# Packed attention and a gated MLP on one core: another order for the first three batches, w_out scaled on VectorE, w_in cast on GpSimd

## The chip, the cores and the metric

The kernel runs on one core of a Trainium2 chip. Its engines work side by side, each through its own queue in order, and wait for one another by semaphores: TensorE (PE: matmuls and transposes; weight loads are shown as PEld), VectorE (DVE), ScalarE (ACT), GpSimd (POOL) and SyncE (SP, which here issues the DMAs). The metric is device time in microseconds, the median of several runs. A profiled execution tells where the time goes.

## What is computed

```python
def sm_attn(qq, kk, vv):
    s = scale * np.matmul(qq, kk.transpose(0, 1, 3, 2))      # scale = 1/8
    a = np.exp(s - np.max(s, axis=-1, keepdims=True))
    return np.matmul(a / (np.sum(a, axis=-1, keepdims=True) + 1e-09), vv)

p_packed = sm_attn(p, k, v)                # q, k, v: 8 batches, 8 heads, 576 x 64; p: 32 x 64 per head
out = sm_attn(q, p_packed, p_packed)       # 576 x 64 per head
x = out.transpose(0, 2, 1, 3).reshape(4608, 512)
h = x @ w_in                               # w_in 512 x 2048
g = h * (1.0 / (1.0 + np.exp(-beta * h)))  # beta: 2048
result = g @ w_out                         # w_out 2048 x 512, all float32
```

Each head's 32 packed rows attend over the 576 rows of k and v; then the 576 rows of q attend over the 32 packed rows. The heads side by side are the 4608 x 512 input of an MLP with a gated activation.

## The kernel before

The work goes batch by batch; matmuls are in bf16 with float32 sums. A batch has 512 rows (the main part) and a remainder of 64, and two batches share a tile of 128 remainder rows.

**Attention of a batch.** `load` (L70) brings k, q or v of a batch to SBUF as float32: one DMA for the main part, two for the remainder. `cast` (L84) makes bf16 of it. `transpose_main` (L95) does 16 transposes on PE into PSUM and one copy on DVE (L104); `transpose_rem` (L109) does the remainders of k and q. `scores1` (L131) gives the scores of p against k and their exp on ACT, `packed` (L159) the sums and the packed rows with their division on DVE. `scores2` (L198) gives the scores of q against the packed rows and exp (L212); `norm2` (L215) sums them, and ACT takes Ln and Exp for the reciprocal; `weights2` (L227) multiplies on DVE and makes A2T.

**MLP of a batch.** `fused_w` (L234), in four blocks n of 512 columns, multiplies the packed rows with w_in, and DVE multiplies the result by beta into W (L249). So h is W against A2T: `mlp_main` (L257), 16 feature tiles of two 512-column matmuls and one Silu on ACT each; `mlp_rem` (L268) does the remainder in two halves. `second` (L290) is the product with w_out: for each of 4 tiles of rows (5 for odd batches) 16 accumulating matmuls, a copy on DVE (L303) and a store. It is a generator: each step is one matmul, and `fill(n)` in `phase` puts n of its steps between other work on PE.

**Phases.** `phase(i)` (L471) holds the MLP mains of batch i, the attention of batch i+1 and, as fill, `second` of batch i-1. It also casts batch i+2 on Pool (`refill`, L484) and then loads batch i+3 into the buffer that came free (each of k, q, v has one float32 and one bf16 buffer). After phase 7 `second(7)` follows alone.

**The opening** is written by hand in `run` (L417). p and beta come by ACT's DMA queue, everything else by SP's. `prepare_p` (L347) doubles p and transposes it; `prepare_beta` (L366) guards beta against zero, takes 1/beta (`rbeta`), and spreads beta over all partitions by 16 float32 matmuls in two halves (`brow_ps`, L385; copies on ACT, L390). w_in and w_out come in four blocks of 1 MB each through a pool `stage` of two buffers (L42), which p32 uses as well. DVE casts each w_in block to bf16 (L400); Pool multiplies each w_out block by rbeta into bf16, in four pieces of 512 columns (L412). The order of `run` sets the order in each queue:

```python
o3 = self.load_w_out(3)      # L457; loads on SP's queue
self.cast_w_out(2, o2)       # Pool
self.cast_w_out(3, o3)
for x in "kqv":
    self.load(1, x)          # L461, SP
for x in "kqv":
    self.cast(1, x, pcopy)   # L463, Pool
```

PSUM for attention, transposes and W is a pool `ps_a` of two buffers that all of them take in turn (`att`, L65); mains use two of `ps_h`, `second` two of `ps_o`.

Of the kernel before, what the change touches and what calls it, by code (L numbers as in the profile page):

```python
# [21 lines left out]
NC = 4  # L22
# [8 lines left out]
class Kernel:  # L31
# [3 lines left out]
    def __init__(self, ctx, tc, q, k, v, p, w_in, w_out, beta, out):  # L35
# [6 lines left out]
        self.stage = pool("stage", 2)  # L42
# [41 lines left out]
    def cast(self, b, x, copy):  # L84
        t = self.x32.pop((b, x))
        o = self.inbf.tile([128, 2304], bf16, tag=f"{x}bf", name=f"{x}_bf")
        copy(  # L87
            o[:, 0:2048].rearrange("p (t h d) -> p h t d", t=4, h=8),
            t[:, 0:2048].rearrange("p (h t d) -> p h t d", h=8, t=4),
        )  # L90
        copy(o[:, 2048:2304], t[:, 2048:2304])
        self.xbf[b, x] = o


    def transpose_main(self, b, x):  # L95
        ps = self.att(f"{x}T_ps", bf16)
        src = self.xbf[b, x]
        for c in range(NC):
# [190 lines left out]

    def second(self, b):  # L290

        nc = self.nc
        for t in range(4 + b % 2):
            ps = self.ps_o.tile([128, DM], f32, tag="o", name="o_ps")
            for ft in range(FT):
                lhsT = (
                    self.g[b][:, ft, 128 * t : 128 * t + 128] if t < 4 else self.grem[b // 2][:, ft, :]
                )
                self.mm(ps[:], lhsT, self.w_out_bf[:, ft, :], start=(ft == 0), stop=(ft == FT - 1))
                if ft < FT - 1:  # L300
                    yield
            o = self.op.tile([128, DM], f32, tag="o_sb", name="o_sb")
            nc.vector.tensor_copy(o[:], ps[:])  # L303
            if t < 4:
                rows = self.out[S * b : S * b + SM, :].rearrange("(p t) n -> p t n", t=4)
                nc.sync.dma_start(rows[:, t, :], o[:])
            else:
                for e in range(2):
                    lo = S * (b - 1 + e) + SM
                    nc.sync.dma_start(self.out[lo : lo + SR, :], o[64 * e : 64 * e + 64, :])  # L310
            yield
# [159 lines left out]
    def phase(self, i):  # L471
# [64 lines left out]
        for _ in w2:  # L536
            pass
# [48 lines left out]
```

## Time and profile before

| | us |
|---|---|
| median of 3 runs (lowest to highest) | 333.84 (333.37 to 334.16) |
| the profiled execution | 333.31 |
| its span, first to last instruction | 331.5 |
| PE busy | 257.6 (78%) |
| ACT busy | 167.7 (51%) |
| DVE busy | 120.4 (36%) |
| POOL busy | 77.4 (23%) |
| mean granted TensorE clock | 0.912 of full speed |

Busy time is that of instructions on the engine; register, branch and semaphore work isn't counted. Matmuls are pipelined, so the mean duration of one is longer than its share of a stream. The granted clock is given as a share of 2.4 GHz: 1.00, or 0.50 for 1.2 GHz. The strip of 40 slices has 8.3 us to a slice, and a digit is the busy share in tenths. In the chain that ended last each step is followed back to what released it.

### The profile page before, as it was taken

The page shows a single profiled execution, that of the slowest core. Times are in us where ns is not written, and L with a number is a line of the kernel's source. Part 1 is how long each engine was busy: PE and PEld are TensorE (multiplying, and loading weights), DVE is VectorE, ACT ScalarE, POOL GpSimd, SP SyncE. Part 2 cuts the span into 40 slices and gives each one's busy share as a digit, 9 for nine tenths or more (in the row PEclk, how much of TensorE's full clock was granted, in tenths as well). Part 3 has the DMA queues.
Part 4 walks back from the last instruction along what each step waited for, and adds up shares of the span by engine and source line. Part 5 has one row for each costly group of instructions (what it writes and reads, how often), then busy time and mean ns, then how long its engine had stood idle before and what let it go on. Part 6 is the DMA issues. An engine that isn't in the chain of part 4 may idle for free.

```text
span 331.5 us, 5201 instructions
## 1 busy us (share of the span) xinstructions
PE 257.6 (78%) x2188; PEld 134.7 (41%) x2225; DVE 120.4 (36%) x155; ACT 167.7 (51%) x242; POOL 77.4 (23%) x69
## 2 busy tenths in 40 slices
PE   0297320006659999999999999999999999999994
PEld 0196100005315544643464365345534543544541
DVE  1433760002225228435433651374236427201111
ACT  1024230000986877587458757862886687443300
POOL 3030008999520520440043005200510000000000
PEclk9999555555969999999999999999999999999999
DMA  8960553599994492097029606912010010111122
GB/s 207 300 237 2 170 203 133 180 339 300 296 291 134 140 296 91 34 304 219 32 49 304 205 34 165 313 47 65 32 44 33 22 65 32 41 56 63 47 83 63
DMA packets 49607, 47.01 MB, mean 142 GB/s; under 512 B 16288, under 2 KB 40880, under 8 KB 49584
## 3 DMA queue, kind: packets, MB, share of 16 engines
q1 hardware_dynamic: 47488, 46.15, 46.8%
q10 hardware_dynamic: 2096, 0.53, 0.9%
q8 instruction: 17, 0.28, 0.4%
q14 instruction: 6, 0.05, 0.1%
HBM read 37.23 MB, written 9.44 MB: 141 GB/s over the span
## 4 chain that ended last, share of the span: by engine, by line
PE 71%; ACT 7%; POOL 7%; DMA 5%; issue 4%; DVE 4%; DVEq 0%; POOLq 0%
PE o_ps L58 34%; PE h_ps L58 18%; POOL w_out_bf L412 7%; PE w_ps L58 4%; DMA p<-in_p_dram 3%; PE kT_ps L63 3%; PE qT_ps L63 3%; PE pp_ps L58 3%; ACT E2T L212 2%; PE brow_ps L58 2%; ACT g_main L266 2%; DMA w_out<-in_moe_w_out_dram 2%; PE z_ps L58 1%; DVE w_in_bf L400 1%; PE s_ps L58 1%
## 5 line engine op out<-in xcount | busy, mean ns | idle before, releaser
L58 PE MATMUL o_ps<-w_out_bf,g_main 128*128 128x512 bf16 x496 | 131.7, 380 | 1.7 <-issue 0.5
L266 ACT ACTIVATE g_main<-h_ps 128x512 bf16<-128x512 f32 x128 | 75.8, 597 | 99.3 <-PE h_ps L58 89.5
L58 PE MATMUL h_ps<-A2T,W_bf 128*128 128x64 bf16 (+1 forms) x494 | 83.7, 288 | 1.2 <-ACT g_main L266 0.7
L58 PEld LDWEIGHTS <-g_main 128*128 128x128 bf16 x512 | 47.9, 98 | 55.6 <-issue 2.7
L303 DVE COPY o_sb<-o_ps 128x512 f32<-128x512 f32 x36 | 24.9, 692 | 103.8 <-PE o_ps L58 103.8
L58 PEld LDWEIGHTS <-W_bf 128*128 128x128 bf16 x512 | 31.1, 98 | 28.3 <-issue 8.3
L249 DVE TENSOR_TENSOR W_bf<-w_ps,beta_bc 128x1024 bf16<-128x1024 f32 x32 | 38.4, 1221 | 10.0 <-PE w_ps L58 9.1
L87 POOL CAST k_bf<-k 128x2048 bf16<-128x2048 f32 x7 | 13.2, 1892 | 97.1 <-issue 81.2
L412 POOL TENSOR_SCALAR w_out_bf<-w_out,rbeta 128x512 bf16<-128x512 f32 x16 | 24.7, 1563 | 31.1 <-DMA w_out<-in_moe_w_out_dram 31.1
L63 PE MATMUL kT_ps<-identr,k_bf 128*128 128x128 bf16 x128 | 10.1, 243 | 27.4 <-POOL k_bf L87 27.3
L104 DVE COPY kT<-kT_ps 128x2048 bf16<-128x2048 bf16 x8 | 9.8, 1225 | 44.5 <-PE kT_ps L63 44.5
L63 PEld LDWEIGHTS <-k_bf 128*128 128x128 bf16 x144 | 10.8, 110 | 31.8 <-POOL k_bf L87 28.2
L58 PE MATMUL w_ps<-w_in_bf,pp 64*32 64x512 bf16 x256 | 14.6, 434 | 11.7 <-DVE w_in_bf L400 10.7
L126 ACT ACT_TABLE_LOAD x15 | 19.2, 1283 | 4.8 <-issue 4.6
L129 ACT ACT_TABLE_LOAD x15 | 19.2, 1283 | 0.3
L87 POOL CAST q_bf<-q 128x2048 bf16<-128x2048 f32 x8 | 15.1, 1894 | 15.1 <-DMA q<-in_q_dram 15.1
L186 DVE RECIPROCAL rz<-pp_ps 128x128 f32<-128x128 f32 x8 | 7.7, 958 | 29.0 <-PE pp_ps L58 29.0
L87 POOL CAST v_bf<-v 128x2048 bf16<-128x2048 f32 x7 | 13.3, 1893 | 20.3 <-issue 18.5
L58 PEld LDWEIGHTS <-pp 64*32 64x32 bf16 x384 | 5.0, 90 | 29.7 <-issue 17.5
L58 PE MATMUL o_ps<-w_out_bf,g_rem 128*128 128x512 bf16 x62 | 14.0, 379 | 0.1
L212 ACT ACTIVATE E2T<-s_ps 128x1024 bf16<-128x1024 f32 (+1 forms) x16 | 9.6, 648 | 6.0 <-PE s_ps L58 5.9
L223 ACT ACTIVATE rz<-z_ps 128x1024 f32<-128x1024 f32 (+1 forms) x16 | 9.5, 648 | 6.2 <-PE z_ps L58 4.0
(60 smaller groups left out, 188.2 us busy)
## 6 DMA issues: line engine op xcount, KB each, us to landing
k<-in_k_dram SPq DMA_DIRECT2D x8, 1024.0 KB, 6.6
v<-in_v_dram SPq DMA_DIRECT2D x8, 1024.0 KB, 8.1
q<-in_q_dram SPq DMA_DIRECT2D x8, 1024.0 KB, 8.6
out_dram<-o_sb SPq DMA_DIRECT2D x32, 256.0 KB, 2.4
w_in<-in_moe_w_in_dram SPq DMA_DIRECT2D x4, 1024.0 KB, 6.4
w_out<-in_moe_w_out_dram SPq DMA_DIRECT2D x4, 1024.0 KB, 5.3
k<-in_k_dram SPq DMA_DIRECT2D x16, 64.0 KB, 6.5
v<-in_v_dram SPq DMA_DIRECT2D x16, 64.0 KB, 6.5
```

Of the source, the lines that this page charges most:

```text
L58: return self.nc.tensor.matmul(out, lhsT, rhs, start=start, stop=stop, tile_position=pos, skip_group_check=True)
L63: return self.nc.tensor.matmul(out, in_, ident, is_transpose=True, skip_group_check=True)
L87: copy(o[:, 0:2048].rearrange("p (t h d) -> p h t d", t=4, h=8), t[:, 0:2048].rearrange("p (h t d) -> p h t d", h=8, t=4),)
L104: self.nc.vector.tensor_copy(xT[:, :, 0:SM], ps[:].rearrange("p (c n) -> p c n", c=NC))
L126: self.nc.scalar.preload_act_table_set(EXP_SET)
L129: self.nc.scalar.preload_act_table_set(SILU_SET)
L212: nc.scalar.activation(E[:, :, lo:hi], ps[:, :, 0 : hi - lo], AF.Exp, scale=SCALE)
L223: nc.scalar.activation(rz[:, :, lo:hi], ps[:, :, 0 : hi - lo], AF.Ln)
L249: self.nc.vector.tensor_tensor(W[:, :, cols], ps, self.beta_bc[:, cols].unsqueeze(1).to_broadcast([128, 2, 512]), ALU.mult,)
L266: self.nc.scalar.activation(self.g[b][:, ft, :], ps[:], AF.Silu)
L303: nc.vector.tensor_copy(o[:], ps[:])
L412: self.nc.gpsimd.tensor_scalar_mul(self.w_out_bf[:, ft, :], t[:, i, :], self.rbeta[:, ft : ft + 1])
```

## The change

- **Loads.** p's buffer is taken from the pool `gp`, `stage` has three buffers, and beta is sent ahead of p. The main parts of k, q and v of batch 0 come in that order, each in two DMAs, then three blocks of w_in at once, the fourth behind the cast of the first, then k, q and v of batch 1, then the blocks of w_out. Two of these are emitted behind the first attention, two behind the last W block; batch 2 follows.
- **Opening of batch 0.** The beta work stands ahead of p's, and its second half (`spread_beta(1)`) behind `packed(0)`. Casts of k, q and v are split in heads between DVE and ACT, the remainder on Pool; the copies of p's, k's and q's transposes are split between DVE and ACT.
- **Weights.** w_in blocks 0 to 2 are cast by Pool, block 3 half by DVE and half by Pool. w_out is scaled by DVE.
- **Batches 0 to 2.** Phases 0 and 1 are written out in `run`. The mains of batch 0 run between its last W blocks; then comes the attention of batch 1 without fill; `second(0)` starts in it, with its first two row tiles interleaved by blocks of w_out, and stands between the mains of batch 1. The attention of batch 2 has 46 steps of `second(1)` as fill; phase 2 takes over its other 34.
- **Phases 2 to 7.** k's transposes stand behind main 2 and q's behind main 4 (before: behind mains 0 and 1). The casts and the loads stand at the head of the phase, with the cast for the batch whose attention is in the same phase.

```diff
--- before.py
+++ after.py
-        self.stage = pool("stage", 2)
+        self.stage = pool("stage", 3)
...
-    def load(self, b, x):
+    def load(self, b, x, parts=1):
...
-        nc.sync.dma_start(
-            t[:, 0:2048].rearrange("p (h e) -> p h e", h=8),
-            src[b, :, 0:SM, :].rearrange("h (p t) d -> p h (t d)", p=128),
-        )
+        n = 8 // parts
+        for i in range(parts):
+            h = slice(n * i, n * i + n)
+            nc.sync.dma_start(
+                t[:, 0:2048].rearrange("p (h e) -> p h e", h=8)[:, h],
+                src[b, h, 0:SM, :].rearrange("h (p t) d -> p h (t d)", p=128),
+            )
...
-    def cast(self, b, x, copy):
+    def cast(self, b, x, *copies):
...
-        copy(
-            o[:, 0:2048].rearrange("p (t h d) -> p h t d", t=4, h=8),
-            t[:, 0:2048].rearrange("p (h t d) -> p h t d", h=8, t=4),
-        )
-        copy(o[:, 2048:2304], t[:, 2048:2304])
+        main = copies[:-1]
+        n = 8 // len(main)
+        for i, copy in enumerate(main):
+            h = slice(n * i, n * i + n)
+            copy(
+                o[:, 0:2048].rearrange("p (t h d) -> p h t d", t=4, h=8)[:, h],
+                t[:, 0:2048].rearrange("p (h t d) -> p h t d", h=8, t=4)[:, h],
+            )
+        copies[-1](o[:, 2048:2304], t[:, 2048:2304])
...
-    def transpose_main(self, b, x):
+    def transpose_main(self, b, x, copies=None):
...
-        self.nc.vector.tensor_copy(
-            xT[:, :, 0:SM], ps[:].rearrange("p (c n) -> p c n", c=NC)
-        )
+        copies = copies or [self.nc.vector.tensor_copy]
+        n = NC // len(copies)
+        for i, copy in enumerate(copies):
+            c = slice(n * i, n * i + n)
+            copy(xT[:, c, 0:SM], ps[:].rearrange("p (c n) -> p c n", c=NC)[:, c])
...
     def second(self, b):
 
-        for t in range(4 + b % 2):
-            ps = self.ps_o.tile([128, DM], f32, tag="o", name="o_ps")
-            for ft in range(FT):
-                lhsT = (
-                    self.g[b][:, ft, 128 * t : 128 * t + 128] if t < 4 else self.grem[b // 2][:, ft, :]
-                )
-                self.mm(ps[:], lhsT, self.w_out_bf[:, ft, :], start=(ft == 0), stop=(ft == FT - 1))
-                if ft < FT - 1:
-                    yield
...
+        groups = [[0, 1], [2], [3]] if b == 0 else [[t] for t in range(4 + b % 2)]
+        for group in groups:
+            ps = {t: self.ps_o.tile([128, DM], f32, tag="o", name="o_ps") for t in group}
+            for n in range(4):
+                for t in group:
+                    for ft in range(4 * n, 4 * n + 4):
+                        self.second_mm(b, t, ft, ps[t])
+                        if ft < FT - 1:
+                            yield
+                    if n == 3:
+                        self.second_out(b, t, ps[t])
+                        yield
...
-        self.p32 = self.stage.tile([128, 16, 64], f32, tag="stage", name="p32")
+        self.b16 = self.const.tile([16, 128], f32, name="b16")
+        nc.scalar.dma_start(self.b16[:], self.beta.rearrange("(f p) -> f p", p=128))
+        self.p32 = self.gp.tile([128, 16, 64], f32, tag="grem", name="p32")
         nc.scalar.dma_start(
             self.p32[:], self.p.rearrange("b (g h) j d -> (h j) (b g) d", g=2)
         )
-        self.b16 = self.const.tile([16, 128], f32, name="b16")
-        nc.scalar.dma_start(self.b16[:], self.beta.rearrange("(f p) -> f p", p=128))
...
-        for r in range(2):
+        for r, copy in enumerate((nc.vector.tensor_copy, nc.scalar.copy)):
             h = slice(64 * r, 64 * r + 64)
-            nc.vector.tensor_copy(
+            copy(
...
-        for half in range(2):
-            ps = self.att("brow_ps")
...
-            nc.scalar.copy(self.beta_bc[:, 1024 * half : 1024 * half + 1024], ps[:])
+        self.b_safe = bs
+
+    def spread_beta(self, half):
+        ps = self.att("brow_ps")
...
+        self.nc.scalar.copy(self.beta_bc[:, 1024 * half : 1024 * half + 1024], ps[:])
...
-    def cast_w_in(self, n, t, copy):
-        copy(self.w_in_bf[:, :, 512 * n : 512 * n + 512], t[:])
+    def cast_w_in(self, n, t, *copies):
+        m = NC // len(copies)
+        for i, copy in enumerate(copies):
+            c = slice(m * i, m * i + m)
+            copy(self.w_in_bf[:, c, 512 * n : 512 * n + 512], t[:, c])
...
-            self.nc.gpsimd.tensor_scalar_mul(
+            self.nc.vector.tensor_scalar_mul(
                 self.w_out_bf[:, ft, :], t[:, i, :], self.rbeta[:, ft : ft + 1]
             )
...
     def run(self):
         nc = self.nc
-        vcopy, scopy, pcopy = nc.vector.tensor_copy, nc.scalar.copy, nc.gpsimd.tensor_copy
-        self.load(0, "k")
+        dve, act, pool = nc.vector.tensor_copy, nc.scalar.copy, nc.gpsimd.tensor_copy
         self.load_small()
-        self.load(0, "v")
-        self.load(0, "q")
+        self.load(0, "k", 2)
+        self.load(0, "q", 2)
+        self.load(0, "v", 2)
+        w = [self.load_w_in(n) for n in range(3)]
+        self.exp_set()
         self.constants()
-        self.exp_set()
+        self.prepare_beta()
+        self.spread_beta(0)
+        self.cast(0, "k", dve, act, pool)
         self.prepare_p()
-        self.prepare_beta()
-        w = self.load_w_in(0)
-        self.cast(0, "k", vcopy)
-        self.transpose_main(0, "k")
-        self.cast(0, "v", scopy)
-        self.cast(0, "q", pcopy)
-        self.transpose_main(0, "q")
+        self.transpose_main(0, "k", [dve, act])
+        self.cast(0, "q", dve, act, pool)
+        self.transpose_main(0, "q", [dve, act])
         self.transpose_rem(0)
         self.scores1(0)
+        self.cast(0, "v", dve, act, pool)
+        self.cast_w_in(0, w[0], pool)
+        w.append(self.load_w_in(3))
+        for x in "kqv":
+            self.load(1, x)
         self.packed(0)
-        w1 = self.load_w_in(1)
-        self.cast_w_in(0, w, vcopy)
+        self.spread_beta(1)
+        self.scores2(0)
         self.fused_w(0, 0)
-        self.scores2(0)
-        w2 = self.load_w_in(2)
-        self.cast_w_in(1, w1, vcopy)
+        self.cast_w_in(1, w[1], pool)
+        self.norm2(0)
         self.fused_w(0, 1)
-        self.norm2(0)
         self.weights2(0)
         self.silu_set()
-        w3 = self.load_w_in(3)
-        self.cast_w_in(2, w2, vcopy)
+        wo = [self.load_w_out(0), self.load_w_out(1)]
+        self.cast_w_in(2, w[2], pool)
+        for ft in range(4):
+            self.mlp_main(0, ft)
         self.fused_w(0, 2)
-        o0 = self.load_w_out(0)
-        self.cast_w_in(3, w3, vcopy)
+        self.cast_w_in(3, w[3], dve, pool)
+        for ft in range(4, 8):
+            self.mlp_main(0, ft)
         self.fused_w(0, 3)
-        o1 = self.load_w_out(1)
-        self.cast_w_out(0, o0)
-        o2 = self.load_w_out(2)
-        self.cast_w_out(1, o1)
-        o3 = self.load_w_out(3)
-        self.cast_w_out(2, o2)
-        self.cast_w_out(3, o3)
+        wo += [self.load_w_out(2), self.load_w_out(3)]
         for x in "kqv":
-            self.load(1, x)
-        for x in "kqv":
-            self.cast(1, x, pcopy)
+            self.cast(1, x, pool, pool)
         for x in "kqv":
             self.load(2, x)
-        for i in range(B):
-            self.phase(i)
-        for _ in self.second(B - 1):
-            pass
-
-    def phase(self, i):
-        w2 = self.second(i - 1) if i > 0 else iter(())
+        for ft in range(8, 12):
+            self.mlp_main(0, ft)
+        self.transpose_main(1, "k")
+        for ft in range(12, 16):
+            self.mlp_main(0, ft)
+        self.mlp_rem(0, 0)
+        self.mlp_rem(0, 1)
+        self.transpose_main(1, "q")
+        self.transpose_rem(1)
+        self.exp_set()
+        self.scores1(1)
+        self.packed(1)
+        self.scores2(1)
+        w2 = self.second(0)
+        self.cast_w_out(0, wo[0])
+        self.fused_w(1, 0)
+        self.norm2(1)
+        self.silu_set()
+        self.fill(w2, 8)
+        self.weights2(1)
+        self.fused_w(1, 1)
+        self.cast_w_out(1, wo[1])
+        for ft in range(4):
+            self.mlp_main(1, ft)
+            self.fill(w2, 1)
+        self.fill(w2, 4)
+        self.fused_w(1, 2)
+        self.cast_w_out(2, wo[2])
+        for ft in range(4, 8):
+            self.mlp_main(1, ft)
+        self.fused_w(1, 3)
+        self.cast_w_out(3, wo[3])
+        self.fill(w2, 8)
+        for ft in range(8, 12):
+            self.mlp_main(1, ft)
+        for ft in range(12, 16):
+            self.mlp_main(1, ft)
+            self.fill(w2, 4)
+        self.mlp_rem(1, 0)
+        self.fill(w2, 4)
+        self.mlp_rem(1, 1)
+        for x in "kqv":
+            self.cast(2, x, pool, pool)
+        for x in "kqv":
+            self.load(3, x)
+        self.fill(w2, 99)
+        w2 = self.second(1)
+        self.fill(w2, 2)
+        self.transpose_main(2, "k")
+        self.fill(w2, 6)
+        self.transpose_main(2, "q")
+        self.fill(w2, 6)
+        self.transpose_rem(2)
+        self.exp_set()
+        self.scores1(2)
+        self.fill(w2, 8)
+        self.packed(2)
+        self.fill(w2, 8)
+        self.scores2(2)
+        self.fill(w2, 8)
+        self.norm2(2)
+        self.silu_set()
+        self.fused_w(2, 0)
+        self.fill(w2, 4)
+        self.fused_w(2, 1)
+        self.weights2(2)
+        self.fused_w(2, 2)
+        self.fill(w2, 4)
+        self.fused_w(2, 3)
+        for i in range(2, B):
+            self.phase(i, w2 if i == 2 else self.second(i - 1))
+        self.fill(self.second(B - 1), 99)
+
...
+    def phase(self, i, w2):
         nb = i + 1
...
         def refill(x):
+            if nb < B:
+                self.cast(nb, x, pcopy, pcopy)
             if nb + 1 < B:
-                self.cast(nb + 1, x, pcopy)
-            if nb + 2 < B:
-                self.load(nb + 2, x)
+                self.load(nb + 1, x)
+
+        for x in "kqv":
+            refill(x)
 
...
         main(0, 2)
+        main(1, 2)
+        main(2, 2)
         attn("transpose_main", nb, "k")
-        main(1, 2)
-        attn("transpose_main", nb, "q")
-        main(2, 2)
-        attn("transpose_rem", nb)
-        refill("k")
-        refill("q")
         main(3, 2)
         main(4, 2)
+        attn("transpose_main", nb, "q")
         main(5, 1)
+        attn("transpose_rem", nb)
         attn("exp_set")
         attn("scores1", nb)
         attn("silu_set")
         fill(14)
         main(6, 2)
         attn("packed", nb)
-        refill("v")
...
```

## Rows read from the trace of the kernel before

**Rows 1.** The page, part 2: busy tenths and granted clock of TensorE, 40 slices.
```profile
PE   0297320006659999999999999999999999999994
...
PEclk9999555555969999999999999999999999999999
```

**Rows 2.** Chain that ended last, in order of time: start, us, what.
```profile
0.71 9.78 DMA p<-in_p_dram
...
11.87 1.90 PE pT_ps L63 x16
...
17.10 7.01 PE brow_ps L58 x32
...
42.90 1.36 DVE A2T L229
...
45.42 5.32 DMA w_out<-in_moe_w_out_dram
...
50.92 21.07 POOL w_out_bf L412 x14
...
77.47 1.89 PE kT_ps L63 x16
```

**Rows 3.** Timeline, SP queue: start, us, engine, line, operation, names, count.
```profile
63.71 0.50 SPq L73 DMA_DIRECT2D k<-in_k_dram  x1
```

**Rows 4.** Windows: stretch, length, busy PE, PEld, DVE, ACT, POOL, clock, DMA, GB/s.
```profile
5.00:11.00 6.00, 0.00 (x0) 0.00 (x0) 0.48 (x1) 0.86 (x1) 0.00 (x0) 1.00 1.19 285
...
17.00:21.00 4.00, 4.00 (x20) 4.00 (x20) 2.88 (x3) 0.27 (x1) 2.87 (x2) 1.00 1.04 389
...
60.00:70.00 10.00, 0.00 (x0) 0.00 (x0) 0.00 (x0) 0.00 (x0) 10.00 (x8) 0.50 0.72 253
...
77.40:82.80 5.40, 5.12 (x38) 4.19 (x40) 2.07 (x2) 0.60 (x1) 4.72 (x6) 0.50 1.09 306
```

**Rows 5.** Timeline of the opening: start, us, engine, line, operation, idle before.
```profile
16.64 1.89 POOL L87 CAST q_bf<-q 128x2048 bf16<-128x2048 f32 x1 [13.03 <-DMA q<-in_q_dram]
...
17.31 2.30 DVE L87 CAST k_bf<-k 128x2048 bf16<-128x2048 f32 x1
...
18.48 1.40 POOL L91 CAST q_bf<-q 128x256 bf16<-128x256 f32 x1
...
25.06 1.90 ACT L87 CAST v_bf<-v 128x2048 bf16<-128x2048 f32 x1
...
28.95 0.63 PE L58 MATMUL s_ps<-pT,kT 128*128 128x64 bf16 x16 [0.89 <-DVE qT L104]
...
32.76 0.96 DVE L186 RECIPROCAL rz<-pp_ps 128x128 f32<-128x128 f32 x1 [3.46 <-PE pp_ps L58]
...
34.39 1.23 DVE L400 CAST w_in_bf<-w_in 128x2048 bf16<-128x2048 f32 x1
...
36.07 0.65 PE L58 MATMUL s_ps<-qT,pp 64*32 64x512 bf16 x8
```

**Rows 6.** Groups by form, 136 to 310 us: busy, mean ns | idle before.
```profile
L266 ACT ACTIVATE g_main<-h_ps 128x512 bf16<-128x512 f32 x94 | 56.1, 597 | 52.6 <-PE h_ps L58 45.6 <-PE qT_ps L63 3.5 <-PE w_ps L58 1.5
...
L249 DVE TENSOR_TENSOR W_bf<-w_ps,beta_bc 128x1024 bf16<-128x1024 f32 x20 | 24.0, 1221 | 0.8
...
L303 DVE COPY o_sb<-o_ps 128x512 f32<-128x512 f32 x27 | 18.7, 692 | 79.3 <-PE o_ps L58 79.3
...
L104 DVE COPY qT<-qT_ps 128x2048 bf16<-128x2048 bf16 x5 | 6.1, 1225 | 2.7 <-PE qT_ps L63 2.7
```

**Rows 7.** Windows of phases 1 and 2 (columns as in rows 4).
```profile
104.75:133.80 29.05, 28.24 (x263) 14.36 (x267) 13.13 (x16) 20.84 (x31) 6.66 (x6) 1.00 0.54 151
...
133.80:166.20 32.40, 31.43 (x279) 15.81 (x282) 13.82 (x17) 20.95 (x31) 6.66 (x6) 1.00 0.51 151
```

**Rows 8.** Timeline of phase 1: the table loaded for Silu.
```profile
124.87 1.28 ACT L129 ACT_TABLE_LOAD   x1
```

**Rows 9.** Chain in order of time: the tail.
```profile
310.96 10.74 PE o_ps L58 x49
```

More of the change, by code (lines that the diff above doesn't have):

```diff
@@ L288, in mlp_rem, with second_mm, second_out @@
         )
-    def second(self, b):
-        nc = self.nc
-        for t in range(4 + b % 2):
-            ps = self.ps_o.tile([128, DM], f32, tag="o", name="o_ps")
-            for ft in range(FT):
-                lhsT = (
-                    self.g[b][:, ft, 128 * t : 128 * t + 128] if t < 4 else self.grem[b // 2][:, ft, :]
-                )
-                self.mm(ps[:], lhsT, self.w_out_bf[:, ft, :], start=(ft == 0), stop=(ft == FT - 1))
-                if ft < FT - 1:
-                    yield
[L302 to L311, printed above, removed]
+    def second_mm(self, b, t, ft, ps):
+        lhsT = self.g[b][:, ft, 128 * t : 128 * t + 128] if t < 4 else self.grem[b // 2][:, ft, :]
+        self.mm(ps[:], lhsT, self.w_out_bf[:, ft, :], start=(ft == 0), stop=(ft == FT - 1))
+    def second_out(self, b, t, ps):
+        nc = self.nc
+        o = self.op.tile([128, DM], f32, tag="o_sb", name="o_sb")
+        nc.vector.tensor_copy(o[:], ps[:])
+        if t < 4:
+            rows = self.out[S * b : S * b + SM, :].rearrange("(p t) n -> p t n", t=4)
+            nc.sync.dma_start(rows[:, t, :], o[:])
+        else:
+            for e in range(2):
+                lo = S * (b - 1 + e) + SM
+                nc.sync.dma_start(self.out[lo : lo + SR, :], o[64 * e : 64 * e + 64, :])
+    def second(self, b):
+        groups = [[0, 1], [2], [3]] if b == 0 else [[t] for t in range(4 + b % 2)]
[10 more added lines that the diff above has]
+                        yield
     def constants(self):
@@ L380, in prepare_beta @@
         nc.vector.reciprocal(self.rbeta[:], pc[:, 0:16])
[L381 to L390 removed]
+        self.b_safe = bs
+    def spread_beta(self, half):
+        ps = self.att("brow_ps")
+        for i in range(8):
+            f = 8 * half + i
+            self.mm(
+                ps[:, 128 * i : 128 * i + 128],
+                self.ident32[0:16, f : f + 1].to_broadcast([16, 128]),
+                self.b_safe[:],
+            )
+        self.nc.scalar.copy(self.beta_bc[:, 1024 * half : 1024 * half + 1024], ps[:])
     def load_w_in(self, n):
@@ L473, in phase, with fill @@
+        self.fused_w(2, 2)
[4 more added lines that the diff above has]
+        self.fill(self.second(B - 1), 99)
+    def fill(self, work, n):
+        for _ in range(n):
+            if next(work, self) is self:
+                break
+    def phase(self, i, w2):
         nb = i + 1
@@ L476, in fill @@
         def fill(n):
-            for _ in range(n):
-                next(w2, None)
+            self.fill(w2, n)
         def attn(f, *a):
@@ L535, in phase @@
         self.mlp_rem(i, 1)
-        for _ in w2:
-            pass
+        fill(99)
 @with_exitstack
```

7 lines of the change are left out of this document (removed).

## Prediction

> **What bounds the kernel now.** I read the strip of 40 slices first. TensorE (PE) is at nine tenths in nearly every slice after 104 us, and there is a pit before: from 33 to 83 us it does almost nothing at the lower granted clock [rows 1]. So the kernel has two parts: an opening that waits and seven phases that are PE-bound. In phase 1 PE is busy 28.24 of 29.05 us, in phase 2 31.43 of 32.40 [rows 7]; nothing on other engines can shorten those much. (A window there begins at the phase's first transposes; the phase itself begins with a main, 0.9 us before.)
>
> The chain of waits names what fills the opening [rows 2]: p's landing (10.5 us), 7.0 us of fp32 matmuls that spread beta, w_in casts up to A2T (44.3), then the first w_out block and 21.07 us of Pool scaling w_out, 14 pieces at 1.5 us, and only then batch 1's cast and the transposes at 77.5. The SP queue says why batch 1 is so late: the fourth w_out load waits for a buffer that Pool frees, and k of batch 1 is queued behind it, issued at 63.71 [rows 3]; while Pool held the queue, DMA ran at 253 GB/s and PE at nothing [rows 4]. Phase 0's order puts batch 1's transposes after main 0, so 15 of 16 mains of batch 0, whose A2T was ready at 44.3, wait until after 77. That hole is what the change can take away.
>
> **The change part by part.** Times are of the profiled span (331.5 us).
>
> *Loads.* In the old order k, v, p and q, 4.06 MB, are in when Pool's q cast starts at 16.64 [rows 5]. k, q and v are 1.18 MB each; at 285 GB/s [rows 4] the last of them took 4.1 us, so with q second q is in at about 12.5. v takes 16.6. w_in comes at up to 389 GB/s [rows 4], 1.05 MB in 2.7 to 3.7 us: the blocks land at about 20, 23, 27 and 30 (the fourth needs only Pool's cast of the first). Batch 1 follows (34, 38, 42) and w_out 0 to 2 (46, 49, 52). A landing is on the path only for p and q.
>
> *Opening to the first main.* p still lands at 10.5 to 11 (beta is sent ahead of it, 8 KB). Doubling and transposing p took 10.5 to 13.8; I take 14.3. The beta spread is halved and, if beta lands before 7, lies in front of p for nothing. k's transposes follow at once (1.89, to 16.2 [rows 2]), copied by DVE and ACT in halves (of 1225 ns [rows 6], so 0.6; on ACT 1.0, half of its 1.90 cast of 2048 columns [rows 5]: 17.1); q's cast in halves 1.0 (18.1), transposes 1.9 (20.0), copy 1.0 (21.0). Scores 1 to the end of packed's matmuls took 28.95 to 32.76 [rows 5], 3.8; ACT now also casts half of v there (1.0): 25.7. The second half of the beta spread, 7.0 / 2 = 3.5 us [rows 2], now stands in PE's queue between packed and scores 2; it covers the 1.6 us of DVE work there and costs 1.9: 29.2. From scores 2 to A2T's end took 36.1 to 44.3, 8.2, with a w_in cast of 1.23 [rows 5] on DVE in it, which goes to Pool, and partly hidden: 7.7. First main at **36.9** (7.4 earlier), its successors unblocked.
>
> *DVE and Pool side by side.* The old trace has one overlap: k's cast on DVE took 2.30 us while Pool cast q, against 1.23 for w_in's cast of the same size with Pool idle, and Pool's 256-column piece took 1.40, where its 2048 columns took 1.89 [rows 5]. The Trainium skill, "SBUF — State Buffer", on the port pair that VectorE and GpSimd share, says one side blocks fully while the other holds it; those two rows agree. By that rule each of the casts shared by DVE and Pool (k, q, v, the fourth w_in block) could add up to 1.1 us; on the path it could hit two, and the sum would be 2 us higher. I take 0 to 2 us and put 0 in the sum, since Pool's share is small pieces. Pool's cast of a w_in block lies between its 1.89 for 2048 columns [rows 5] and 4 x 1.5 for the scaling [rows 2]; even 6 us a block ends at 42, ahead of need, so it costs nothing.
>
> *Batch 0's MLP, 36.9 to 51.* Sixteen mains at 0.43 PE (two matmuls at 0.22 [rows 9]) or 0.86 at the lower clock, ACT 0.60 each [rows 6]. The clock rose at 82.8, after PE had been busy 5.12 of 5.40 us [rows 4]; I let the first six mains run at 0.86 (5.2), ten at 0.60 (6.0), two W blocks 1.0, k's transposes 0.9, two remainders 1.2: end 51.2.
>
> *Attention of batch 1 without filler.* q's transposes end at 52; s1 needs q's copy 1225 ns [rows 6], 53.3; then 3.3 to packed's end, 1.6 DVE, s2 and exp: second(0) gets its first fill only behind norm2, at about 61.6. Of these 10 us some 3 are work, so 7 stay lost; I let the clock fall in it and the next 5 us run at half speed (8 fills 3.4 instead of 1.7).
>
> *w_out on DVE.* Four pieces a block; the unknown price of a piece is between 1.23 / 4 = 0.3 and the 0.69 of a 512-column PSUM copy [rows 5, 6]; I take 0.4, 1.6 a block. Blocks 0 and 1 stand in front of W multiplies (1.22 each [rows 6]), and fills wait for block 1 (to 68.5); at 0.69 this adds 2 us. Blocks 2 and 3 are covered by mains. The fourth load waits for block 0's scaling (59.5) and lands 5.3 us later [rows 2], before its need at 75; batch 2's loads behind it land by 75, need 89.
>
> *Second(0) with MLP 1.* From 61.6: 8 fills 3.4; W and mains with block 1 to 70.4; W, four mains, W 3.2; 8 fills 1.8; four mains 2.4; four mains with 16 fills 5.2; two remainders and 24 fills 6.1: **89.3**. Then second(1) is opened and 46 of its 80 fills go beside batch 2's attention: 46 x 0.219 + 6.4 of attention matmuls + 1.3 stalls at the W multiplies: phase 2 starts at **107** (old 133.0, the piece before the transposes at 133.8).
>
> *Phase 2* has 34 fills left instead of 80. Up to scores 2 it uses the 32 it always used; then ACT sets the pace. In phase 1, begun at 103.9, the silu table was loaded by 126.15 [rows 8], 22.2 us on, with nothing before it that the missing fills shorten; eight silus at 0.60 follow [rows 6]: 27.0 instead of 32.4 [rows 7], 5.4 off.
>
> *Phases 2 to 6, moved transposes.* q's transposes now stand one main ahead of scores 1; its PSUM buffer is free after DVE's 1225 ns copy, PE arrives after 0.65 + 0.23: 0.4 to 0.5 us of stall per phase, 2.0 in four phases (phase 2's is in the 27). Moving casts and loads to the head of the phase costs nothing: their inputs are done in the phase before, and output stores are queued behind loads that don't wait. Between 0 (hidden) and 0.9 per phase.
>
> **Sum.** Phase 3 begins at 134 instead of 165.3: 331.5 - 31.3 + 2.0 = 302.2 us of span. The profiled execution took 333.31, 1.8 over its span: 304.0; the median of the runs is 0.5 above it: **304.5 us**.
>
> **Rivals.**
> *The opening is slower than my chain* (0.24, about 311): the clock falls again in batch 2's attention (2.7), mains run at 0.86 longer (3), DVE pieces at 0.69 (2). For: in the slice from 91.2 to 99.5 the clock was down again for part of it, between two at full, in an attention with few fills [rows 1]. Against: after that it never fell.
> *The opening is faster* (0.16, about 299): beta is in early, DMA runs at 389 GB/s throughout, s1's stall is hidden behind fills, the clock is up by 40. Each is worth 1 to 2 us.
> *The loads bind instead* (0.07, about 309): if batch 1 and w_out move at 253 GB/s or less [rows 4], batch 1 lands 4 us later and w_out 2 to 3 some 5 later, which pushes scores 1 and the first fills.
> *Clock stuck, slower than before* (0.02, 370): if pauses between mains, fills and attention keep the granted clock at its lower level from 37 until phase 3, the 65 to 75 us of PE work there double. It needs over 30 us of such work at half speed to lose the whole gain; the strip shows it up for good from 100 us on [rows 1].
> *The change does not do what it says* (0.01, 334): batch 1's loads again stuck behind a weight load. They now stand ahead of w_out and behind the fourth w_in block, whose buffer Pool frees at 22.
>
> **How the numbers follow.** The forecast case has 0.50. The range 297 to 315 holds it with its bounds (unknown DVE pieces +2, port +2, moved transposes -2 to +2) and most of the slower and faster openings and the loads. A measurement tells 0.2%, 0.7 us, from no change: faster 0.97, within 0.01, slower 0.02.
>
> **What would show it.** PE's strip has no empty slices between 37 and 51; batch 1's k is issued before 32; the first fill stands at 58 to 65; phase 2's start near 107, phase 3's near 134; a phase from 3 on 0.4 to 0.5 us longer; Pool's w_in cast near 1.9; a DVE w_out piece near 0.4. Wrong would be: a first main after 42, a second(0) that waits for w_out landings, or steady phases longer by over 1 us.

## The result and the profile after

| | before | after |
|---|---|---|
| median of 4 runs (lowest to highest), us | 334.0 (333.37 to 334.23) | 305.76 (305.26 to 308.15) |
| profiled execution, its span | 333.31, 331.5 | 305.92, 304.1 |
| PE, DVE, ACT, POOL busy | 257.6, 120.4, 167.7, 77.4 | 261.4, 126.0, 165.4, 60.2 |

The ratio is 0.9172 (95%: 0.9122 to 0.9221): faster by 28.2 us, against a forecast of 304.5. A second set of the same two kernels on another chip, used below, gave 307.29 (306.35 to 308.92) against 333.76, so differences of 1 to 2 us between runs of different chips tell little. The work on PE is nearly the same; where it stands is not. The page of after, from its part on busy tenths (answering [rows 1]; a slice is now 7.6 us):

```profile
span 304.1 us, 5209 instructions
...
PE   2768496587999889689999999999999999999993
...
POOL 3136550015206206202600152005200000000000
...
PEclk9999999789999999989999999999999999999998
```

The three empty slices in the pit are gone; what is left is one at 4 tenths just ahead of the first main (30 to 38 us) and one at 5 tenths from 53 to 61 us, the attention of batch 1 without fill, with the granted clock down in it. Pool's solid block of scaling is gone too. The chain of waits, in order of time (start, us, what), answers [rows 2]:

```profile
1.21 8.33 DMA p<-in_p_dram
...
24.21 3.72 PE brow_ps L58 x16
...
34.58 1.77 DVE A2T L239
...
36.39 3.34 PE h_ps L58 x8
...
44.85 1.05 PE kT_ps L63 x16
...
50.35 1.24 DVE qT L116
...
51.63 0.64 PE s_ps L58 x16
...
70.64 3.23 DVE w_out_bf L436 x4
```

Neither a w_out transfer nor Pool is on it any more. A2T ends at 36.35 (44.3 before), batch 1's transposes start at 44.85 (77.47 before). The SP queue's timeline shows why: k of batch 1 is issued at 22.61, at 63.71 in [rows 3].

```profile
22.61 0.44 SPq L76 DMA_DIRECT2D k<-in_k_dram  x1
```

From the first main to the first main of phase 3 the kernel now takes 98.9 us (36.4 to 135.3), and from there to the end 168.8, against 166.3 before (its first main of phase 3 stands at 165.2): the whole gain is made ahead of phase 3, and 2.5 us of it go back later.

### The profile page after: what moved, and what is told of

It reads as the page before. It is cut to its first block, busy times and chain, and to the rows that moved or that the text cites. A ratio compares the mean times of both kernels' runs of the same rounds, so it can differ in the third digit from the quotient of the medians.

```text
span 304.1 us, 5209 instructions
## 1 busy us (share of the span) xinstructions
PE 261.4 (86%) x2189; PEld 135.0 (44%) x2225; DVE 126.0 (41%) x168; ACT 165.4 (54%) x242; POOL 60.2 (20%) x58
## 4 chain that ended last, share of the span: by engine, by line
PE 76%; DVE 8%; ACT 8%; issue 4%; DMA 3%; ACTq 0%
PE o_ps L58 38%; PE h_ps L58 19%; PE w_ps L58 4%; PE pp_ps L58 3%; DMA p<-in_p_dram 3%; PE kT_ps L63 3%; DVE qT L116 3%; PE qT_ps L63 2%; ACT g_main L276 2%; ACT E2T L222 2%; DVE W_bf L259 2%; PE s_ps L58 2%; PE z_ps L58 1%; PE brow_ps L58 1%; DVE w_out_bf L436 1%
## 5 line engine op out<-in xcount | busy, mean ns | idle before, releaser
L58 PE MATMUL o_ps<-w_out_bf,g_main 128*128 128x512 bf16 x491 | 130.1, 383 | 4.0 <-DVE w_out_bf L436 2.4
L276 ACT ACTIVATE g_main<-h_ps 128x512 bf16<-128x512 f32 x128 | 75.0, 596 | 69.2 <-PE h_ps L58 62.6
L58 PEld LDWEIGHTS <-W_bf 128*128 128x128 bf16 x512 | 31.9, 98 | 39.7 <-issue 18.3
L116 DVE COPY kT<-kT_ps 128x2048 bf16<-128x2048 bf16 (+1 forms) x8 | 9.3, 1158 | 18.4 <-PE kT_ps L63 18.4
L58 PE MATMUL o_ps<-w_out_bf,g_rem 128*128 128x512 bf16 x64 | 15.3, 379 | 0.0
L116 DVE COPY qT<-qT_ps 128x2048 bf16<-128x2048 bf16 (+1 forms) x8 | 9.3, 1157 | 13.6 <-PE qT_ps L63 13.6
L95 POOL CAST q_bf<-q 128x2048 bf16<-128x2048 f32 x7 | 13.3, 1907 | 6.5 <-DMA q<-in_q_dram 6.5
L151 ACT ACTIVATE E1T<-s_ps 128x1024 bf16<-128x1024 f32 x8 | 8.2, 1023 | 9.4 <-PE s_ps L58 9.3
L294 ACT ACTIVATE g_rem<-h_ps 128x512 bf16<-128x512 f32 x16 | 9.3, 596 | 6.0 <-PE h_ps L58 5.6
```

Source lines behind the costliest of these rows:

```text
L58: return self.nc.tensor.matmul(out, lhsT, rhs, start=start, stop=stop, tile_position=pos, skip_group_check=True)
L95: copy(o[:, 0:2048].rearrange("p (t h d) -> p h t d", t=4, h=8)[:, h], t[:, 0:2048].rearrange("p (h t d) -> p h t d", h=8, t=4)[:, h],)
L116: copy(xT[:, c, 0:SM], ps[:].rearrange("p (c n) -> p c n", c=NC)[:, c])
L276: self.nc.scalar.activation(self.g[b][:, ft, :], ps[:], AF.Silu)
L294: self.nc.scalar.activation(self.grem[b // 2][:, 8 * half : 8 * half + 8, o : o + 64], ps[:].rearrange("p (f n) -> p f n", f=8), AF.Silu,)
```

## Experiments

Two theories stood against each other. *The hole*: the gain is that batch 1 no longer waits behind w_out's scaling. *The engines*: the gain is that Pool's slow scaling went to DVE and that casts were shared out. Then came the question what the pieces that looked costly are worth, and whether the order written out by hand is the best one.

**Loads alone (on the kernel before).**

```diff
         w3 = self.load_w_in(3)
+        for x in "kqv":
+            self.load(1, x)
+        for x in "kqv":
+            self.cast(1, x, pcopy)
...
-        for x in "kqv":
-            self.load(1, x)
-        for x in "kqv":
-            self.cast(1, x, pcopy)
```

> The kernel before with one edit: k, q and v of batch 1 are loaded behind the fourth w_in block, ahead of w_out, and Pool casts them ahead of its w_out scaling; everything else, Pool's 25 us of scaling among it, stays. Theory (the gain is the hole: batch 1 was queued behind a w_out load that waited for Pool): batch 1's first transposes at about 50 us instead of 77.5, and the loop of phases starts 27 us earlier; phase 1 then waits some 5 us for batch 2's casts, which stand behind the scaling on Pool. Median 309 to 313 us, some three quarters of the change's gain. Rival (the gain needs the scaling on DVE, the split casts and the phases written out): Pool's scaling still has to end before phase 1 can fill, and the time stays above 325.

Measured 316.04 us, ratio 0.9481 (0.944 to 0.9522): moving these lines gives 17.5 of the 28.2 us. Its chain:

```profile
50.12 9.12 DMA w_out<-in_moe_w_out_dram
59.33 22.77 POOL w_out_bf L412 x15
...
84.18 1.91 POOL k_bf L87
86.13 1.89 PE kT_ps L63 x16
```

Batch 1's transposes stand at 51.54 here; the block of Pool scaling is still there, but it lies beside mains and attention. What the expectation missed is that w_out's transfer now comes behind batch 1's, so the scaling ends at 82.1 and holds back batch 2: k's transposes of batch 2 wait 8.5 us for Pool's cast. The hole theory holds, for the larger part. The other 10.7 us were not taken apart. PE's waits for DVE's casts of w_in, 12.3 us here and 10.7 in the kernel before, are gone in the changed kernel, and so is the 8.5 us wait; but no run moves the split casts, the cast of w_in on Pool or the order of the opening by itself, so what each of them brings is not shown.

**w_out scaled on Pool (on the changed kernel).**

```diff
-            self.nc.vector.tensor_scalar_mul(
+            self.nc.gpsimd.tensor_scalar_mul(
```

> The changed kernel with w_out scaled by Pool again (four pieces of 1.5 us a block) at the same place of the order. Theory (order, not engine, matters; DVE's pieces cost what they collide with): Pool is free from 44 us, does the blocks by 50, 56, 63 and 69, each ahead of its need at 60, 66, 72 and 78, and DVE loses 10 us of work, two waits of PE of 1.2 us each and a late W multiply: 2 to 3 us faster than the changed kernel, 303 to 304. Rival (the move to DVE is part of the gain): PE waits for Pool's pieces and the time is 3 us or more above 305.8.

Measured 306.26 us, 0.9186 (0.9153 to 0.9219): no different from the changed kernel. The tile's row (min, median, max ns; first and last start) and the window from the end of phase 2's Silu table load to phase 3's first main (columns as in [rows 4]):

```profile
L436 POOL TENSOR_SCALAR w_out_bf<-w_out,rbeta x16: 1561/1568/2527, 46.1 to 70.1; 128x512 bf16<-128x512 f32 x16
```

```profile
127.95:133.93 5.98, 5.53 (x57) 2.11 (x57) 4.06 (x4) 4.06 (x9) 0.00 (x0) 0.72 1.12 296
```

A piece takes three times as long on Pool, yet no matmul waits for w_out, where PE waits 2.4 us for it in the changed kernel, and batch 2's transposes come 2.55 us earlier (86.71 against 89.26), as expected. That is more than executions of one kernel differ: the four profiles whose code is the same up to there (the changed kernel, its repeat and the two runs with the transposes back, all below) have them at 89.26, 92.23, 89.26 and 89.91. In the profiled execution half of the gain goes in phase 2, which took 28.85 us instead of 27.69. The loss lies behind the Silu table: the stretch above took 5.98 us at a granted clock of 0.72, where the same stretch of the changed kernel (130.50 to 135.32) took 4.82 at 0.89. The medians show none of the gain; that the clock takes the rest in the other runs too is argued, not shown. What is settled: the engine that scales w_out is not where the gain comes from, once nothing queues behind it.

**Batch 1 behind w_out (on the changed kernel).** The loop `self.load(1, x)` moves from behind `load_w_in(3)` to between `load_w_out(2)` and `load_w_out(3)`:

```diff
-        for x in "kqv":
-            self.load(1, x)
...
-        wo += [self.load_w_out(2), self.load_w_out(3)]
+        wo.append(self.load_w_out(2))
+        for x in "kqv":
+            self.load(1, x)
+        wo.append(self.load_w_out(3))
```

> The changed kernel with the loads of batch 1 behind the first three w_out blocks instead of ahead of them. Theory (the place of batch 1 in SP's queue counts by what it waits for there): the third w_out block waits for the cast of the fourth w_in block, at about 42 us, so k of batch 1 is issued at 42.5 instead of 22.6, lands at 48 to 49, and its transposes wait for the cast until about 51 instead of 44.9 with eight mains behind them: 5 to 7 us slower than the changed kernel, 311 to 313. Rival (the loads of batch 1 have slack, and the gain is in what the engines do): within 1.5 us of 306.

Measured 315.51 us, 0.9467 (0.9424 to 0.9509), 9.8 us slower (8.2 against the second set's 307.29). The waits of the SP queue and of PE (who, for whom, us in total, times, longest), and then the SP timeline:

```profile
SPq L428 <- DVE w_in_bf L424: 10.7, 1, 10.7
...
PE kT_ps L63 <- POOL k_bf L95: 8.1, 1, 8.1
```

```profile
41.67 0.46 SPq L76 DMA_DIRECT2D k<-in_k_dram  x1
```

The third w_out load waits for a buffer that the last w_in cast frees, and batch 1 queues behind it: the mechanism of the kernel before, with another cast at its head. Scores 1 come 8.9 us later (60.53), and nothing makes it up: the first fill stands at 70.14 (9.7 later), batch 2's transposes at 97.41 (8.2 later). The expectation had the size too small. Both directions thus show that what stands in front of batch 1 in SP's queue decides the larger part.

**Transposes of phases 2 to 6 back in their old places (on the changed kernel), twice.**

```diff
         main(0, 2)
+        attn("transpose_main", nb, "k")
         main(1, 2)
+        attn("transpose_main", nb, "q")
         main(2, 2)
-        attn("transpose_main", nb, "k")
+        attn("transpose_rem", nb)
         main(3, 2)
         main(4, 2)
-        attn("transpose_main", nb, "q")
         main(5, 1)
-        attn("transpose_rem", nb)
```

> The changed kernel with k's and q's transposes of phases 2 to 6 back behind mains 0 and 1 and the remainders behind main 2. Theory: the 0.45 us wait of scores 1 for q's copy on DVE goes in all five phases: 2.0 to 2.3 us faster, about 303.6. Rival: the wait is slack that another takes up (ACT or the copies of k and q), and the time stays within 0.5 us of 305.8.

Measured 305.69 us, 0.917 (0.9148 to 0.9192), which tells nothing by itself, though its phases were shorter. So the kernel ran again beside the unchanged after on one chip:

> The changed kernel once more, on one chip with the three that follow, since the medians of its variants lie within the spread of its own runs (305.26 to 308.15). All theories: 305 to 307 us; it is what the other three are held against.

> The changed kernel with the transposes of phases 2 to 6 back at mains 0 and 1, again, beside the changed kernel on the same chip. Its profile showed the steady phases at 28.9 and 32.4 us instead of 29.5 and 33.0, which is 2.4 us over four phases. Theory: 2 to 2.5 us faster than the changed kernel of this set. Rival (another part gives it back, such as a fall of the granted clock in the opening or in phase 2): within 0.7 us of it.

Measured 307.29 us, 0.9214 (0.9187 to 0.924), for the changed kernel and 304.82, 0.9139 (0.9111 to 0.9168), with the transposes back: 2.5 us, with intervals that don't touch. (The first run, 305.69, had no unchanged kernel beside it.) PE's waits in the changed kernel from 134.7 us on name the four stalls (us in total, times, longest); with the transposes back no such row is left in that part:

```profile
PE s_ps L58 <- DVE qT L116: 1.8, 4, 0.4
```

From phase 3 on, the phases take 29.53 and 32.99 us in turn in the changed kernel, 28.93 and 32.38 with the transposes back (start to start of k's transposes), as before the change; both profiles of either kernel agree to 0.01. The starts of phases 3 and 4, first in the changed kernel, then with the transposes back:

```profile
137.91 1.06 PE L63 MATMUL kT_ps<-identr,k_bf 128*128 128x128 bf16 x16
...
167.44 1.06 PE L63 MATMUL kT_ps<-identr,k_bf 128*128 128x128 bf16 x16
```

```profile
137.55 1.06 PE L63 MATMUL kT_ps<-identr,k_bf 128*128 128x128 bf16 x16
...
166.48 1.06 PE L63 MATMUL kT_ps<-identr,k_bf 128*128 128x128 bf16 x16
```

Moving them cost 0.61 a phase, 2.4 over four. That the medians differ by nearly the same is weaker evidence: up to batch 2's transposes, in code that the two kernels share, the two profiles of this chip already differ by 2.3 us.

**The second half of the beta spread behind A2T (on the changed kernel).**

```diff
-        self.spread_beta(1)
         self.scores2(0)
...
         self.silu_set()
+        self.spread_beta(1)
```

> The changed kernel with the second half of the beta spread (16 fp32 matmuls) moved from behind packed(0) to behind weights2(0), where PE waits 3.1 us for A2T. Theory (it stands on the path of the opening): scores 2 starts 2.0 us earlier, A2T is ready at about 34.4, the spread takes 3.7 us of PE from about 31.5 on and so ends close to A2T: 1 to 2 us faster, 304 to 304.8. Rival (it is hidden, or takes the place of mains): within 0.4 us of 305.8, or slower by 1 to 2 where the mains wait for it.

Measured 305.58 us, 0.9164 (0.914 to 0.9188): not told apart from the changed kernel. PE's timeline (start, us, what), first of this kernel, then of the changed one:

```profile
35.02 3.59 PE L58 MATMUL h_ps<-A2T,W_bf 128*128 128x512 bf16 x8
38.55 0.63 PE L58 MATMUL w_ps<-w_in_bf,pp 64*32 64x512 bf16 x8
39.10 2.72 PE L58 MATMUL h_ps<-A2T,W_bf 128*128 128x512 bf16 x7
```

```profile
36.39 3.34 PE L58 MATMUL h_ps<-A2T,W_bf 128*128 128x512 bf16 x8 [3.11 <-DVE A2T L239]
39.66 0.41 PE L58 MATMUL w_ps<-w_in_bf,pp 64*32 64x512 bf16 x8
40.00 1.04 PE L58 MATMUL h_ps<-A2T,W_bf 128*128 128x512 bf16 x4
```

The first main comes 1.37 us earlier, as expected, but after its first eight matmuls seven more take 2.72 us (0.39 each), where the changed kernel's next four take 1.04 (0.26). The first fill of `second(0)` stands at 60.51 against 60.47: between these two executions the start was won and the slow matmuls gave it back. That the edit makes them slow isn't shown: the repeat of the changed kernel has nearly as many without it (14, see the end), and in the three other profiles that share the changed kernel's opening the first fill stands at 62.09, 62.56 and 62.95. What is settled is the median: no gain that can be told.

**Phases 0 and 1 by the loop.** If the hole was a matter of order, the hand-written middle need not be the best order. Here all W blocks of batch 0 stand ahead of the first main (blocks 2 and 3 of w_in cast on Pool), and the mains and everything behind them are left to `phase`, for i = 0 too, so that batch 1's attention stands between batch 0's mains and `second(0)` is fill in phase 1. In phase 0 the fill is a generator that scales w_out's pieces on DVE at given steps, and behind the fourth piece issues w_out's last load and batch 2's.

```diff
-        self.cast_w_in(3, w[3], dve, pool)
+        self.cast_w_in(3, w[3], pool)
...
-        for i in range(2, B):
-            self.phase(i, w2 if i == 2 else self.second(i - 1))
+        wo = [self.load_w_out(n) for n in range(3)]
+        for i in range(B):
+            self.phase(i, self.second(i - 1) if i else self.scale_w_out(wo))
...
+    def scale_w_out(self, wo):
+        at = [11, 12, 13, 14, 27, 28, 29, 30, 32, 33, 34, 35, 52, 53, 54, 55]
...
-            if nb + 1 < B:
+            if 0 < i < B - 2:
```

> The changed kernel with its loads, split casts and weight casts, but with phases 0 and 1 run by the same loop as the others: batch 1's attention lies between the mains of batch 0, second(0) and batch 2's attention lie in phase 1, second(1) is whole in phase 2. All four W blocks of batch 0 are done ahead of its first main, and DVE scales w_out in pieces between phase 0's steps. Theory (the written-out part loses what it fills badly: 10 us of batch 1's attention beside nothing and two stretches at the lower clock): first main at 36.5, phase 0 takes 25 us since ACT sets its pace, phase 1 29.5, phase 2 33.0, so phase 3 begins at about 124 instead of 135: 294 to 297 us. Rival (writing phases 0 and 1 out is what gains): phase 1 waits for w_out's last block or for batch 2's casts, and the time is 304 or more.

Measured 298.96 us, 0.8967 (0.8946 to 0.8989): 6.8 us below the changed kernel's 305.76 and 8.3 below the 307.29 on the same chip, but above the expected 294 to 297: phase 0 took 28.1 us in the profile (36.66 to 64.76, first main to first main), not 25, and phase 3 begins at 127.3, not 124. The order written out by hand is thus worse, as a whole, than the loop's. Then with the transposes in their old places in all phases (the diff above):

> The kernel with phases 0 and 1 by the loop, and with the transposes of all phases back at mains 0 and 1. Theory: 0.6 us less in each of phases 1 to 6, and up to 3 us lost in phase 0, where q's transposes then wait for Pool's cast of q (39.6): 1 to 3 us faster than the loop with the later transposes, 292 to 295. Rival: the loss in phase 0 takes all of it: within 0.7 us.

Measured 295.56 us, 0.8863 (0.8843 to 0.8883), 3.4 us faster than the loop before, a little more than expected, though the time is above the 292 to 295 named. Its chain runs through w_out's last pieces:

```profile
57.78 1.23 DVE W_bf L259
59.00 1.66 DVE w_out_bf L436 x3
60.66 1.27 DVE A2T L239
61.93 1.15 DVE W_bf L259
...
63.11 0.41 PE w_ps L58 x8
```

Pieces that nobody needs before phase 1 stand in DVE's queue ahead of A2T and the next W multiply, for which PE's last W block waits. So they move behind them:

```diff
-        at = [..., 52, 53, 54, 55]
-        for step in range(56):
+        at = [..., 60, 61, 62, 63]
+        for step in range(64):
```

> The kernel with phases 0 and 1 by the loop and the transposes at mains 0 and 1, with one more edit: DVE scales the last w_out block behind the first half of phase 0's remainder instead of between its first W multiply and A2T, where its profile showed the chain running through 1.66 us of it. Theory: 1 to 2 us faster than 295.56, as DVE's chain of W multiplies sets the end of phase 0. Rival: ACT or the landing of the next loads ends last there: within 0.5 us.

Measured 294.31 us, 0.8822 (0.8808 to 0.8837), the best version found: 39.7 us under the kernel before and 11.5 under the changed one. Of the 1.25 us that the last edit brings in the medians, which come from two chips, the profile shows 0.3: phase 1's first main stands at 65.77 instead of 66.06, since A2T, now without the pieces in front of it, took 2.43 us beside Pool's cast of k instead of 1.34. Two windows of it, phase 0 and phase 1 (columns as in [rows 4]):

```profile
37.20:66.20 29.00, 22.53 (x202) 11.24 (x202) 19.70 (x30) 20.59 (x30) 10.33 (x9) 0.74 1.07 320
...
66.50:95.50 29.00, 28.39 (x266) 14.24 (x265) 13.24 (x17) 20.78 (x31) 8.95 (x8) 1.00 0.45 127
```

Phase 1 is as full as in [rows 7] from the start. What is still open is phase 0: 22.5 of 29 us busy at a granted clock of 0.74, with nothing of `second` to fill it.

## Why the prediction came out right, step by step

| step | predicted | measured |
|---|---|---|
| p landed; Pool's remainder of q starts | 10.5 to 11; 12.5 | 9.56; 13.75 |
| first main | 36.9 | 36.39 |
| end of batch 0's MLP; scores 1 | 51.2; 53.3 | 49.4; 51.63 |
| first fill of `second(0)` | 61.6 | 60.47 |
| first main of phase 2 | 107 | 107.63 |
| first main of phase 3 | 134 | 135.3 |
| phases 3 to 6, each | +0.4 to 0.5 | +0.61 (phases 3 to 5) |
| span | 302.2 | 304.1 |

*What bounds the kernel.* Right, and shown from both sides: loads alone brought 17.5 us, and batch 1 behind w_out took 9.8 back. The other 10.7 us were forecast step by step and came at the places below, but no run tells them apart by cause.

*Loads and the opening.* Right within 1.3 us at each place. The second half of the spread took 3.72 us (3.5) and stands in front of scores 2 as worked out; taken away there, it gave the first main 1.4 us (1.9 in the sum), which were worth nothing at the end: that the step did not see. (The prediction's "7.4 earlier" is held against A2T's end; the first main of the kernel before stands at 49.13, behind its last W blocks.)

*Batch 0's MLP* was mis-sized by 1.3 us: after the first eight matmuls the rest came at the faster rate, where six mains (12 matmuls) were put at the lower. Two mains at 0.86 instead of 0.60 are 0.5 of it; the rest is W blocks, transposes and remainders, which took less than the sum gave them.

*Attention of batch 1 without filler* took 8.8 us from scores 1 to the first fill (8.3), and the eight fills behind it 3.26 (3.4): the loss and the slow rate after it are as forecast.

*DVE and Pool side by side* was put at nothing, in the wrong place. Most shared casts of the opening were unhurt; it fell on w_out's blocks 2 and 3, which the prediction called covered, and on A2T. The timelines of DVE and Pool (a row of x4 is four pieces in a stretch):

```profile
34.49 1.84 DVE L239 TENSOR_TENSOR A2T<-E2T,rz 128x1152 bf16<-128x1152 bf16 x1
...
56.63 1.67 DVE L436 TENSOR_SCALAR w_out_bf<-w_out,rbeta 128x512 bf16<-128x512 f32 x4
...
70.55 3.30 DVE L436 TENSOR_SCALAR w_out_bf<-w_out,rbeta 128x512 bf16<-128x512 f32 x4
...
71.59 1.99 POOL L95 CAST q_bf<-q 128x2048 bf16<-128x2048 f32 x1 [1.82 <-DMA q<-in_q_dram]
...
73.91 1.24 PE L58 MATMUL o_ps<-w_out_bf,g_main 128*128 128x512 bf16 x5 [1.17 <-DVE w_out_bf L436]
```

With Pool idle a block takes 1.67 us, near the 1.6 of the prediction; beside Pool's cast of q 3.30, and beside that of v 3.43. That is 1.6 to 1.8 more a block, and PE waits 1.17 for the third one. (Its other wait for w_out, 1.21, is for block 1, whose pieces ran with Pool idle behind a W multiply, as the sum has it.) A2T, begun at 34.49 beside Pool's cast of batch 1's k (33.24 to 35.13), took 1.84 against 1.36 in [rows 2].

*Second(0) with MLP 1* was 28.3 us long (27.7), the waits for w_out in it; the terms of the sum add up to 89.1 and not 89.3. *The attention of batch 2* took 18.8 (17.7). The work was right: PE is busy 16.48 us of it, 16.5 in the sum. The waits were not: 2.3 instead of 1.3. The two largest are 1.05 for ACT's part of `norm2` and, ahead of the first main of phase 2, 0.85 for A2T; the sum had only stalls at the W multiplies.

```profile
88.83:107.63 18.80, 16.48 (x180) 8.89 (x182) 10.31 (x14) 6.28 (x9) 6.60 (x6) 1.00 0.82 228
```

```profile
103.30 0.41 PE L58 MATMUL w_ps<-w_in_bf,pp 64*32 64x512 bf16 x8 [1.05 <-ACT rz L233]
```

*Phase 2* was 0.7 longer (27.7 for 27.0), and all of it lies ahead of the eight mains at its end. The wait of scores 1, the Silu table, and the window from there to phase 3 (columns as in [rows 4]):

```profile
115.21 0.63 PE L58 MATMUL s_ps<-pT,kT 128*128 128x64 bf16 x16 [0.45 <-DVE qT L116]
```

```profile
129.22 1.28 ACT L139 ACT_TABLE_LOAD   x1
```

```profile
130.50:135.32 4.82, 4.40 (x57) 1.98 (x57) 3.79 (x4) 3.90 (x8) 0.00 (x0) 0.89 1.13 321
```

The table is loaded at 130.50, 22.9 us after the phase's first main (22.2 in the sum); the rest takes 4.82, as worked out (8 x 0.60), though the clock is at 0.89. The 22.2 was read from a phase of the kernel before, where the transposes had their old places, and so the stall of the moved ones was not "in the 27", as the prediction says: the 0.45 us here come on top. The remaining 0.2 is not taken apart.

*Moved transposes.* The stall at scores 1 is there, 0.45 four times, just as worked out; 0.16 a phase more was not seen.

That the span comes out within 1.9 us is partly luck: it was 1.1 us early at the first fill, 1.3 late at phase 3, 1.9 at the end, so early steps paid for late ones. With other signs the errors would still have left the time well inside 297 to 315. Of the rivals, the stuck clock, the binding loads and a change without effect are ruled out by the strip, the SP row and the first fill. Of the slower opening's terms none came as described: the clock stayed at 1.00 in batch 2's attention (the window above), fewer mains ran at the lower rate (four in this profile), and a piece on DVE took 0.42 alone; it was Pool beside DVE that made pieces dear.

## What to carry to other kernels

Read from the profile what a load waits for and then everything queued behind it: one buffer wait in an in-order queue held back a whole batch, and a few moved lines alone brought 17.5 of the 28.2 us. Where work is moved off a path, ask what follows it in each queue it enters; pieces with no deadline stood for 1.66 us in front of A2T on the chain that ended last, and a faster engine for w_out bought nothing that could be measured over the slower one that had time. Before ordering an opening by hand, try to let the steady loop begin one phase earlier: its filler is worth more than a hand-tuned gap (11.5 us here, with the moved transposes put back).

## What the runs showed of the hardware

*The granted clock at the start of a trace.* In the changed kernel the first eight 512-column matmuls took 3.34 us (0.42 each), and in the repeated run of the same kernel 3.57. The windows of those stretches read:

```profile
36.40:39.50 3.10, 3.10 (x8) 0.91 (x7) 0.00 (x0) 1.55 (x3) 2.39 (x3) 1.00 1.14 305
```

```profile
36.80:40.30 3.50, 3.50 (x13) 0.91 (x13) 0.00 (x0) 1.79 (x3) 2.42 (x3) 0.50 1.14 298
```

One reads 1.00 and the other 0.50 for nearly the same durations; a matmul of that shape takes 0.22 at full speed [rows 9]. So in the opening the durations tell the rate, and the column doesn't always.

*One kernel, two openings.* The changed kernel's batch 2 transposes stood at 89.26 in one profile and at 92.23 in the other, with the same phases from there on. Of the 3 us, 0.4 lie ahead of the first main, 1.6 between it and batch 1's transposes, and 0.5 each in batch 1's attention and in `second(0)`. In the 1.6 two things differ. One is how many mains ran at the lower rate; in the second profile there are six more matmuls at 0.39 behind the first eight:

```profile
40.84 2.35 PE L58 MATMUL h_ps<-A2T,W_bf 128*128 128x512 bf16 x6
```

The other is who came first, DVE or Pool, in the cast of w_in's last block beside Pool's cast of v (first profile, then second):

```profile
41.28 0.68 DVE L424 CAST w_in_bf<-w_in 128x1024 bf16<-128x1024 f32 x1
...
41.28 2.44 POOL L95 CAST v_bf<-v 128x2048 bf16<-128x2048 f32 x1 [1.73 <-ACT g_main L276]
```

```profile
41.83 1.89 POOL L95 CAST v_bf<-v 128x2048 bf16<-128x2048 f32 x1 [1.88 <-DMA v<-in_v_dram]
42.13 2.15 DVE L424 CAST w_in_bf<-w_in 128x1024 bf16<-128x1024 f32 x1
```

In the first both start within 0.01 us; DVE's cast took 0.68 and Pool's 2.44, 0.55 longer than its 1.89. In the second Pool began 0.3 us earlier and took 1.89, and DVE's took 2.15, 1.47 longer. One of the two is at its own speed, the other pays. This is the rule of the Trainium skill, "SBUF — State Buffer", section "SBUF: two separate sides": of a VectorE instruction in a two-port mode and a GpSimd one, whichever starts first holds the shared port pair for its whole instruction, and the other blocks. Which mode DVE's cast ran in, no row tells. The second profile agrees in its order; the first can't show who was ahead. The same skill's "TensorE: Matmul & The Clock Gate", Part 1, says that the number of matmuls at the lower rate differs from run to run of one kernel; the two profiles agree (8 against 14).
